# Two attentions on one core: the first use's small tile grows from 32 to 64 bytes, and every tile above it moves by 32

## The chip, the core and the metric

The kernel runs on one core of one Trainium2 chip. The metric is the device time of one execution in microseconds; a figure for a kernel is the median of its runs. Nothing else runs on the core.

## What is computed

Two attention layers with 32 heads of 18 features each, on separate inputs of 2048 rows and 576 features, all in float32. The first (A) is local and dilated: each position looks at 8 positions, 2 apart, behind it. The second (B) is a full softmax attention over all 2048 positions. Each has its own projection to q, k and v and its own output projection, and the two results stand side by side in the output.

```python
def _A_ref(x, wqkv, wo):            # W, dil = 8, 2
    q, k, v = heads(x @ wqkv)
    idx = pos[:, None] - off[None, :]               # off = arange(8) * 2
    logits = einsum("bhsd,bhswd->bhsw", q, k[idx]) * scale   # -1e9 where idx < 0
    return merge(einsum("bhsw,bhswd->bhsd", softmax(logits), v[idx])) @ wo

def _B_ref(x, wqkv, wo):
    q, k, v = heads(x @ wqkv)
    p = softmax(einsum("bhqd,bhkd->bhqk", q, k) * scale)
    return merge(einsum("bhqk,bhkd->bhqd", p, v)) @ wo

return concatenate([A, B], axis=-1)
```

## The kernel before

**Projections.** Operands are split into a high and a low part so that three products in a fast format stand for one in float32. First comes a third of B's q and k columns (L572), then half of B's values (L316), then the rest and all of A's columns in one list of products (L379, inside `stream`). The results go to DRAM and come back in the layout that the next part wants.

**Full attention (B).** It runs in 8 groups of 4 heads; a group has 4 blocks of 512 queries, and a block has 16 steps of 128 keys. A group's q and k lie in a *set*: a tile `qs` and a tile `ks` of 16,384 bytes in each partition. There are three sets, made by `make_set`, and group g uses set g modulo 3. For each pair of queries and keys the scores are made twice:

- L160, in `take`: a product of q and k whose maxima VectorE takes (L168, in `reduce`, out of the PSUM bank into the small tile `mx`). They run about a group ahead; the maxima are transposed, split (`mt`, `mh`) and loaded as two more rows into `qs` (`place`).
- L284, in `score`: the same product with the maximum's rows, now below zero, which ScalarE exponentiates (L292) into a tile `e` of 128 x 512 float32. The keys are the weights, and `qs` is what moves through TensorE.
- L767, in `weigh`: four products of the step's four `e` tiles (moving) with `v` (weights) add up in the bank `po`, one in each quarter of TensorE's columns. A product in plain float32 stands in the trace as two matmuls, so a step shows 8 records.

`finish` divides by the sums; the output projection follows in sums of a few products in between (L1245, L1213, L1177, and at the very end L890).

**Local attention (A)** is done by GpSimd beside B: products of `aq` with windows of `akv` (L988), sums (L992), the exponentials' products with v's windows (L1030) and their sums (L1031 to L1033). Its output projection (L1348) is put between the scores.

**What sets the order.** The instruction order is written by hand: a step's work plus what an agenda (`plan`, `later`) has due in it. Loads and stores are almost all issued from SyncE's queue (L424 and others), some from ScalarE's and GpSimd's. Tiles come from pools; a pool opened with `side="right"` is laid from the high end of a partition's memory, the others one behind another from the low end.

**Where the tiles lie.** From the low end: 8192 bytes that the kernel reserves (L1462), 128 bytes of small constants, `ones` (512 bytes), two tiles `m` of 128 bytes, then set 0 (two tiles of 16,384). That adds up to 41,856, which is 654 times 64. The pool `maxes` begins there, and its first tile is `warm`, of 32 bytes:

```python
    warm = maxes.tile([2, 8], F32, name="warm", bufs=1)     # L397
    nc.scalar.activation(warm, ones[:, :8], AF.Exp)         # L398
```

This instruction is the first use of ScalarE's table of exponentials (the table's load stands in front of it); nothing reads `warm`. Behind it lie `mx`, `v` of even groups, `mt` and `mh`; then, by stages, `first` (the first inputs), the values, sets 1 and 2, half of the `e` tiles (pool `es`), and the pool `work` with the other `e` tiles, `o`, `n`, `y`, `v` of odd groups and all tiles of A. Each takes a multiple of 64 bytes, so that each lies 32 bytes past a multiple of 64. The tiles laid from the high end (inputs `x`, their rows `raw` and `more`, the projections' weights, `ohi`, `olo`) also lie 32 bytes past a multiple of 64, because the high end does.

Of the kernel before, what the change touches and what calls it, by code (L numbers as in the profile page):

```python
# [7 lines left out]
F32 = mybir.dt.float32  # L8
F32R = mybir.dt.float32r
BF16 = mybir.dt.bfloat16  # L10
AF = mybir.ActivationFunctionType
# [50 lines left out]
def two_attentions(ctx: ExitStack, tc, xa, wa, woa, xb, wb, wob, out):  # L62
# [5 lines left out]
    nc = tc.nc  # L68
# [5 lines left out]
    maxes = ctx.enter_context(tc.tile_pool(name="maxes", bufs=1))  # L74
# [24 lines left out]
    ones = const.tile([2, 128], F32, name="ones")  # L99
# [294 lines left out]

    every = slice(0, 512)

    warm = maxes.tile([2, 8], F32, name="warm", bufs=1)  # L397
    nc.scalar.activation(warm, ones[:, :8], AF.Exp)  # L398

    with (tc.tile_pool(name="x", bufs=1, side="right") as xp,  # L400
          tc.tile_pool(name="a0", bufs=1, side="right") as a0):
# [1068 lines left out]
```

## Time and profile before

| | us |
|---|---|
| runs | 1581.26, 1583.42, 1583.88 |
| median | 1583.42 |
| the profiled execution, its own time | 1582.18 |
| its span, from the first to the last instruction | 1579.8 |

The profile is of one execution; its own time is 2.38 us more than its span, and 1.24 us less than the median of the runs. A line of a group of instructions gives the source line, engine, operation, tiles (output <- inputs, without buffer numbers) and shapes, the count, then busy time in us and the mean duration of one in ns, then the engine's idle time in front of them and what ended it. PEld is TensorE's loading of weights, which goes on beside its matmuls. Ends of matmuls are modelled, so that a busy TensorE can hide short waits; the time from one group of steps to the next is the sturdier number.

### The profile page before, as it was taken

How to read it: one execution, taken by the hardware profiler on the slowest of the kernel's cores; microseconds unless marked ns; L12 is line 12 of the kernel's file. 1: busy time of each engine (PE TensorE's matmuls, PEld its weight loads, DVE VectorE, ACT ScalarE, POOL GpSimd, SP SyncE). 2: the span in 40 equal slices, each digit the busy share in tenths (PEclk: the TensorE clock that was granted, in tenths of full speed). 3: DMA queues.
4: the chain of work that ended last, by engine and by line, in shares of the span. 5: the costliest groups of instructions: out<-in, count | busy, mean ns of one | idle time of the engine just before them, and what ended most of it. 6: DMA issues, size and time to landing. Idle time of an engine off the chain costs nothing.

```text
span 1579.8 us, 34955 instructions
## 1 busy us (share of the span) xinstructions
PE 1570.8 (99%) x13272; PEld 940.6 (60%) x13272; DVE 1380.6 (87%) x2333; ACT 1207.4 (76%) x2411; POOL 970.7 (61%) x803
## 2 busy tenths in 40 slices
PE   9999999999999999999999999999999999999998
PEld 7998888999544445445445445444444444545686
DVE  5299999999999999999989999999999999988633
ACT  6424441121699999999999999999999999998654
POOL 2415752210166996996896897797798799682000
PEclk9999999999999999999999999999999999999999
DMA  8948854532312362245326324421721332144311
GB/s 248 241 137 210 270 165 132 145 106 76 66 35 71 71 141 70 73 119 111 74 74 134 90 79 121 118 79 50 152 82 50 91 95 58 50 165 132 140 57 69
DMA packets 188168, 175.65 MB, mean 111 GB/s; under 512 B 119432, under 2 KB 133512, under 8 KB 186272
## 3 DMA queue, kind: packets, MB, share of 16 engines
q1 hardware_dynamic: 182992, 161.73, 36.9%
q0 software_dynamic: 4032, 10.63, 3.2%
q8 instruction: 104, 1.70, 0.5%
q10 hardware_dynamic: 976, 1.07, 0.2%
q14 instruction: 64, 0.52, 0.1%
HBM read 98.77 MB, written 73.47 MB: 109 GB/s over the span
## 4 chain that ended last, share of the span: by engine, by line
PE 97%; DVE 3%; DMA 0%; issue 0%; ACT 0%; SPq 0%; DVEq 0%
PE po L767 30%; PE bank L284 19%; PE bank L160 18%; PE bank L379 17%; PE bank L1348 4%; PE bank L1245 3%; PE bank L572 2%; PE bank L316 2%; DVE mx L168 2%; PE bank L1213 0%; DMA first<-xb 0%; PE bank L1177 0%; PE bank L890 0%; DVE am L1005 0%; DVE o L782 0%
## 5 line engine op out<-in xcount | busy, mean ns | idle before, releaser
L168 DVE TENSOR_REDUCE mx<-bank 128x2 f32<-128x512 f32 x2048 | 1281.8, 684 | 108.4 <-PE bank L160 82.0
L292 ACT ACTIVATE e<-bank 128x512 f32<-128x512 f32 x2048 | 1047.6, 603 | 80.8 <-PE bank L284 78.7
L160 PE MATMUL bank<-ks,qs 54*128 54x512 f32 (+1 forms) x2464 | 787.8, 380 | 2.2 <-DVE mx L168 0.9
L160 PEld LDWEIGHTS bank<-ks,qs 54*128 54x128 f32 x2464 | 402.8, 184 | 392.6 <-DVE mx L168 341.8
L284 PE MATMUL bank<-qs,ks 56*128 56x512 f32 x2048 | 591.3, 425 | 0.6 <-ACT ohi L716 0.6
L767 PE MATMUL po<-e,v 128*19 128x512 f32 x4096 | 531.7, 598 | 0.4
L284 PEld LDWEIGHTS bank<-qs,ks 56*128 56x128 f32 x2048 | 308.7, 184 | 20.8 <-ACT e L292 14.1
L988 POOL TENSOR_TENSOR pr<-aq,akv 128x1024 f32<-128x1024 f32 x72 | 158.5, 2202 | 17.1 <-PE bank L160 14.3
L1030 POOL TENSOR_TENSOR pr<-lg,akv 128x1024 f32<-128x1024 f32 x72 | 158.3, 2199 | 0.6
L767 PEld LDWEIGHTS po<-e,v 128*19 128x19 f32 x4096 | 73.6, 97 | 138.5 <-issue 133.2
L992 POOL TENSOR_TENSOR pr<-pr 128x1024 f32<-128x1024 f32 x64 | 152.7, 2385 | 5.0
L716 ACT ACTIVATE ohi<-bank 128x512 f32<-128x512 f32 (+1 forms) x56 | 30.4, 595 | 151.9 <-issue 126.4
L379 PE MATMUL bank<-xlo,ahi 64*128 64x512 f32 (+1 forms) x448 | 123.5, 387 | 0.0
L379 PE MATMUL bank<-xhi,alo 64*128 64x512 f32 (+1 forms) x448 | 118.7, 387 | 0.0
L379 PE MATMUL bank<-xhi,ahi 64*128 64x512 f32 (+1 forms) x448 | 112.9, 387 | 0.0
L1348 PE MATMUL bank<-wohi,at 64*128 64x288 f32 x480 | 103.3, 304 | 0.0
L1031 POOL TENSOR_TENSOR pr<-pr 128x512 f32<-128x512 f32 x72 | 92.4, 1284 | 5.6
L431 POOL TENSOR_TENSOR alo<-raw,ahi 128x512 fp32r<-128x512 f32 (+1 forms) x14 | 17.6, 1256 | 121.8 <-ACT ahi L430 115.4
L1348 PEld LDWEIGHTS bank<-wohi,at 64*128 64x128 f32 x480 | 74.6, 184 | 27.6 <-ACT e L292 23.8
L526 POOL TENSOR_TENSOR olo<-olo,ohi 128x512 fp32r<-128x512 f32 x36 | 46.2, 1294 | 68.9 <-ACT ohi L525 58.6
L103 POOL CAST mh<-mt 128x32 fp32r<-128x32 f32 x32 | 6.8, 212 | 113.7 <-DVE mt L185 113.7
L379 PEld LDWEIGHTS bank<-xlo,ahi 64*128 64x128 f32 (+1 forms) x448 | 72.0, 182 | 6.0
(210 smaller groups left out, 1866.9 us busy)
## 6 DMA issues: line engine op xcount, KB each, us to landing
do<-n SPq DMA_DIRECT2D x30, 512.0 KB
da<-ohi SPq DMA_DIRECT2D x52, 256.0 KB
akv<-da SPq DMA_DIRECT2D x64, 175.5 KB
out<-y SPq DMA_DIRECT2D x31, 288.0 KB
qs<-dqk SPq DMA_DIRECT2D x30, 288.0 KB
ks<-dqk SPq DMA_DIRECT2D x30, 288.0 KB
at<-dao SPq DMA_DIRECT2D x60, 128.0 KB
rec<-drec SPq DMA_DIRECT2D x29, 256.0 KB
```

The costliest lines, as they stand in the source:

```text
L160: return awaiting(nc.tensor.matmul(ps if part is None else ps[:, 256 * r : 256 * r + 256], qs[at, b, p, 128 * t : 128 * t + 128], ks[at, p ...
L168: nc.vector.tensor_reduce(at, ps.rearrange("q (s n) -> q s n", s=2), axis=AX.X, op=ALU.max)
L284: awaiting(nc.tensor.matmul(ps, ks[at, p, 128 * kt : 128 * kt + 128], qs[at, b, p], start=True, stop=True))
L292: nc.scalar.activation(e, ps, AF.Exp, scale=SCALE)
L379: nc.tensor.matmul(ps, a, b, start=start, stop=stop)
L767: nc.tensor.matmul(po[32 * i : 32 * i + 19], vs[g][:, kt, 19 * i : 19 * i + 19], es[i], start=kt == 0, stop=kt == NT - 1)
L988: nc.gpsimd.tensor_mul(pr, ap(st["q"][:, 2 * c], (SUB, 2), (0, W), (1, SUB)), window(st["k"], c))
L992: nc.gpsimd.tensor_add(st["pr"], st["pr"], pr)
L1030: nc.gpsimd.tensor_mul(at, ap(st["lg"], (0, 2), (SUB, W), (1, SUB)), window(st["v"], c))
L1031: nc.gpsimd.tensor_add(at[:, :, :4], at[:, :, :4], at[:, :, 4:])
L1245: nc.tensor.matmul(sums_[r], *both[r][i], start=i == 0, stop=last)
L1348: return nc.tensor.matmul(ps, a, b, start=r == k == 0, stop=r == 1 and k == len(both[1]) - 1)
```

## The change

`warm` becomes a tile of 16 elements, 64 bytes, and the activation fills all of it:

```diff
-    warm = maxes.tile([2, 8], F32, name="warm", bufs=1)
-    nc.scalar.activation(warm, ones[:, :8], AF.Exp)
+    warm = maxes.tile([2, 16], F32, name="warm", bufs=1)
+    nc.scalar.activation(warm, ones[:, :16], AF.Exp)
```

Every tile behind `warm` from the low end moves up by 32 bytes, onto a multiple of 64: `mx`, `v`, `mt`, `mh`, `first`, the values, sets 1 and 2, all `e` tiles, and all of `work`. What lies in front of it stays, set 0 among them, which already lay on a multiple of 64; what is laid from the high end stays too, 32 bytes past one. The shift is the same for all that move, so distances among them are kept.

On ScalarE, at the very start of the program, the order of instructions reads like this (a minus is the kernel before, a plus the changed one; `first` is the room for the first inputs):

```order
 L1466 UNCONDITIONAL_BRANCH
 L398 ACT_TABLE_LOAD
-L398 ACTIVATE warm<-ones 2x8
+L398 ACTIVATE warm<-ones 2x16
 L424 DMA first<-xb 128x512
 L424 DMA first<-wb 128x2x192
```

No instruction moves: the activation is longer by 8 elements on 2 partitions, and every other row, on every engine, is the same in both, with the same waits.

## The prediction

> **What bounds the kernel now.** I read the page's shares and chain first, to see whose time counts; then the groups; then one stretch for each group of heads, because the kernel before already holds both kinds of tile: set 0 on a multiple of 64 bytes, sets 1 and 2 32 bytes past one. The page:
>
> ```profile
> span 1579.8 us, 34955 instructions
> ...
> PE 1570.8 (99%) x13272; PEld 940.6 (60%) x13272; DVE 1380.6 (87%) x2333; ACT 1207.4 (76%) x2411; POOL 970.7 (61%) x803
> ...
> PE 97%; DVE 3%; DMA 0%; issue 0%; ACT 0%; SPq 0%; DVEq 0%
> PE po L767 30%; PE bank L284 19%; PE bank L160 18%; PE bank L379 17%; PE bank L1348 4%; PE bank L1245 3%; PE bank L572 2%; PE bank L316 2%; DVE mx L168 2%; PE bank L1213 0%; DMA first<-xb 0%; PE bank L1177 0%; PE bank L890 0%; DVE am L1005 0%; DVE o L782 0%
> ```
>
> TensorE is busy for 99% of the span and carries 97% of the chain of waits; transfers, ScalarE and GpSimd carry about nothing. So a tile's place is worth something only if it changes what TensorE takes for a matmul, or makes another engine late enough to stop it. The groups that could:
>
> ```profile
> L168 DVE TENSOR_REDUCE mx<-bank 128x2 f32<-128x512 f32 x2048 | 1281.8, 684 | 108.4 <-PE bank L160 82.0
> L292 ACT ACTIVATE e<-bank 128x512 f32<-128x512 f32 x2048 | 1047.6, 603 | 80.8 <-PE bank L284 78.7
> ...
> L284 PE MATMUL bank<-qs,ks 56*128 56x512 f32 x2048 | 591.3, 425 | 0.6 <-ACT ohi L716 0.6
> L767 PE MATMUL po<-e,v 128*19 128x512 f32 x4096 | 531.7, 598 | 0.4
> ```
>
> Of what moves, TensorE reads sets 1 and 2 (L284, L160), `e` and `v` (L767) and the late tiles of the output projections. Its matmuls on `x` and the weights (L379, L572, L316) read tiles of the high end, which stay.
>
> **The change part by part.**
>
> *The longer activation.* It stands at the very start:
>
> ```profile
> 2.03 0.21 ACT L398 ACTIVATE warm<-ones 2x8 f32<-2x8 f32 x1
> ...
> 4.28 0.52 ACT L430 ACTIVATE whi<-first 128x384 fp32r<-128x384 f32 x1 [2.04 <-DMA first<-wb]
> ```
>
> It takes 0.21 us and ends at 2.24; ScalarE then idles 2.04 us for a transfer. Eight more elements on two partitions cost far less than that: 0. Without the cover it could cost at most what it takes now, 0.2 us.
>
> *Scores and maxima (L284, L160) on sets 1 and 2.* Each block of 16 steps reads rows of 512 elements of `qs`. Groups 3 to 6 have the same work for TensorE (1161 to 1163 matmuls), and use sets 0, 1, 2 and 0 for the scores. These are the stretches of the four groups, each from its first score to the next group's, with every engine's busy time:
>
> ```profile
> core 0: us, PE busy (x) PEld busy (x) DVE busy (x) ACT busy (x) POOL busy (x), PEclk, DMA share, GB/s
> 817.40:958.00 140.60, 140.49 (x1163) 68.50 (x1159) 129.96 (x220) 134.40 (x267) 121.63 (x88) 1.00 0.42 102
> 958.00:1098.30 140.30, 140.21 (x1161) 68.06 (x1157) 129.83 (x221) 133.99 (x266) 115.78 (x83) 1.00 0.35 90
> 1098.30:1239.00 140.70, 140.36 (x1161) 68.14 (x1157) 131.34 (x226) 134.53 (x267) 107.84 (x81) 1.00 0.39 93
> 1239.00:1379.90 140.90, 140.40 (x1161) 67.94 (x1157) 129.55 (x221) 134.10 (x266) 122.96 (x97) 1.00 0.26 73
> ```
>
> And the score matmuls alone (L284) in the same stretches:
>
> ```profile
> 817.40:958.00 140.60, 75.64 (x256) 39.47 (x256) 1.00 0.42 102
> 958.00:1098.30 140.30, 75.48 (x256) 39.29 (x256) 1.00 0.35 90
> 1098.30:1239.00 140.70, 75.44 (x256) 39.34 (x256) 1.00 0.39 93
> 1239.00:1379.90 140.90, 75.34 (x256) 39.30 (x256) 1.00 0.26 73
> ```
>
> The two groups on the aligned set take 140.6 and 140.9 us, the two on shifted sets 140.3 and 140.7. The means differ by 0.25 us, the wrong way for a gain, and less than like groups differ from each other (0.3 and 0.4). Loading `ks` as weights takes 39.3 to 39.5 us in all four. The group on 140.3 is the one in which scores and maxima both mostly read shifted sets, so the maxima hide nothing either. Five groups (1, 2, 4, 5, 7) get an aligned set by the change. The pairs of aligned less shifted go from 140.6 - 140.7 = -0.1 to 140.9 - 140.3 = +0.6 us a group, so the bounds are 5 x -0.1 = -0.5 and 5 x 0.6 = +3.0 us. I take 0, because the scatter among equals covers the difference.
>
> *The products with `e` and `v` (L767).* No `e` lies on a multiple of 64 in this trace. The nearest row is L284, where `qs` also moves through TensorE in rows of 2048 bytes: aligned less shifted goes from 75.34 - 75.48 = -0.14 to 75.64 - 75.44 = +0.20 us on 75.5, that is -0.19% to +0.27%. On 531.7 us that makes -1.0 to +1.4. I take 0, the middle of those rows. `v` is the weights, whose loading lies beside the matmuls.
>
> *What the other engines do with moved tiles.* VectorE's results go 8 bytes at a time to all places of `mx`. GpSimd's windows of `akv` begin, from product to product, 624 bytes on, so that they take four different places within 64 bytes. The rows of these (min/median/max in ns):
>
> ```profile
> L168 DVE TENSOR_REDUCE mx<-bank x2048: 623/682/696, 81.8 to 1491.0; 128x2 f32<-128x512 f32 x187
> ...
> L988 POOL TENSOR_TENSOR pr<-aq,akv x72: 2185/2202/2217, 427.7 to 1329.4; 128x1024 f32<-128x1024 f32 x72
> ...
> L1030 POOL TENSOR_TENSOR pr<-lg,akv x72: 2180/2198/2218, 511.8 to 1404.6; 128x1024 f32<-128x1024 f32 x72
> ```
>
> The 72 products differ by 1.5% from the fastest to the slowest, so the place of an operand is worth no more than that there, and GpSimd is on no chain. VectorE's maxima stand at 682 wherever they go. For both I take 0. ScalarE's writing of `e` has no aligned counterpart; it is a rival below. It is covered as long as ScalarE has time left: in group 3 it is busy 134.4 of 140.6 us, which leaves 6.2 us for 256 activations, 24 ns each.
>
> *Transfers.* The chain holds one, the first inputs into `first`, a tile that moves:
>
> ```profile
> 0.97 3.98 DMA first<-xb
> ```
>
> The loads into `ks` from GpSimd's queue, for set 0 (at 56 us), set 1 (at 159) and set 2 (at 281), land like this:
>
> ```profile
> DMA to landing us min/median/max: 10.5/12.7/14.8
> ...
> DMA to landing us min/median/max: 5.8/6.0/6.8
> ...
> DMA to landing us min/median/max: 4.7/5.9/6.4
> ```
>
> The aligned set is the slowest, because it loads while the other inputs do; sets 1 and 2 lie alike and land alike. A price for the place can't be seen under the load's. The nearest rows for a bound are the medians of sets 1 and 2, which lie alike and differ by 0.1 in 6: on 3.98 us that is 0.07 us either way. I take 0.
>
> On that row the Trainium skill has a rule against this change: "DMA: Bandwidth & Descriptors", section "How a descriptor splits into AXI transactions", says that a descriptor is fetched from the boundary of 256 bytes below its start, and that what lies between costs beats of 32 bytes. By that page a tile that moves up by 32 bytes, and not onto a multiple of 256, costs a beat more for each row: for a row of `y` of 2304 bytes, 72 beats, some 1.4% (an estimate from the page). No run here shows it; by that rule stores get longer that nothing on the chain waits for, and the sum stays the same.
>
> **The sum.** Against the profiled execution's own 1582.18 us (1579.8 of span and 2.38 around it): 0 + 0 + 0 + 0 + 0, so 1582.2. That execution lies 1.2 below the median of the three runs; the middle of all four times (1581.26, 1582.18, 1583.42, 1583.88) is 1582.8, and that is the forecast.
>
> **The rivals.**
>
> *Faster: rows are fetched in pieces of 64 bytes.* A row of 2048 bytes that begins 32 past a multiple touches 33 such pieces, an aligned one 32. If TensorE's reading of `e` were bound by that, L767 would fall by a 33rd: 531.7 / 33 = 16.1 us, and the time would be 1566.7. For it speaks only that no aligned `e` was ever seen. Against it: the same 33rd would be 75.5 / 33 = 2.3 us a group between sets 0 and 1 or 2 in L284, where the rows differ by 0.2 at most, in both directions. 0.11.
>
> *Slower: ScalarE becomes the bound.* If an activation that writes `e` to a multiple of 64 is longer, 24 ns each are hidden, as worked out above (4% of 603); from there on every ns costs 2048 ns. At 30 ns more that is 6 x 2048 = 12.3 us, so 1595. For it: ScalarE is the second busiest engine of these stretches, and this trace shows no wide write of ScalarE at such a place. Against it: no operand on any engine shows a price of place of even 2%. 0.09.
>
> *The change doesn't do what it says:* tiles of the high end remain 32 bytes past a multiple, so that matmuls on `x` keep whatever they pay. They are 21% of the chain (L379, L572 and L316). But those rows hold no sign of a price either, and without one this rival's time is the forecast's, 1582.8. 0.02.
>
> **How the numbers follow.** The forecast, no change beyond scatter, has 0.78. A measurement of this kernel tells about 0.2% (3.2 us) from no change: three runs alone spread over 2.6 us. With the third rival, "within 0.2%" gets 0.80, faster 0.11, slower 0.09. The range takes the bounds: below 1582.8 - 0.5 (scores) - 1.0 (`e`) - 1.5 (from the middle down to the fastest run) = 1579.8; above 1582.8 + 3.0 + 1.4 + 1.1 (up to the slowest run) = 1588.3. I set 1579 to 1588; what is left out are the first two rivals, 0.2 together.
>
> **What would show it.** Right: the four stretches of groups again at 140 to 141 us, L284 again near 75.5 in each, now without a difference of kind; L767 near 531.7 busy; L292 at 603 ns; the chain still 97% TensorE. L767 down to about 516 would prove the first rival; L292 at 627 or more, with ScalarE in the chain, the second. The forecast is wrong if the groups that used set 1 and 2 change and groups 3 and 6 don't, or if all eight change alike: that would be a price of `e`, `v` or `mx` that no row of this trace could show.

## The result, and the profile after

| | before | after |
|---|---|---|
| median of 20 runs, us | 1582.81 | 1585.74 |
| range, us | 1580.93 to 1588.03 | 1584.77 to 1589.31 |
| profiled execution, own time / span | 1582.18 / 1579.8 | 1585.33 / 1583.5 |

The ratio is 1.0019, with a 95% interval of 1.0013 to 1.0026. The change costs 2.9 us. That lies inside the predicted range, but it is more than scatter, and the forecast was none.

The page of the changed kernel, with the rows that answer to those shown of before:

```profile
span 1583.5 us, 34955 instructions
...
PE 1573.9 (99%) x13272; PEld 939.6 (59%) x13272; DVE 1382.0 (87%) x2333; ACT 1207.7 (76%) x2411; POOL 969.8 (61%) x803
...
PE 95%; DVE 3%; DMA 1%; ACT 0%; issue 0%; POOL 0%; SPq 0%; DVEq 0%; POOLq 0%; ACTq 0%
PE po L767 30%; PE bank L284 19%; PE bank L160 18%; PE bank L379 16%; PE bank L1348 4%; PE bank L1245 3%; PE bank L572 2%; PE bank L316 2%; DVE mx L168 2%; DMA raw<-xa 1%; PE bank L1213 0%; ACT e L292 0%; DMA first<-xb 0%; DMA dqk<-olo 0%; PE bank L1177 0%
...
L168 DVE TENSOR_REDUCE mx<-bank 128x2 f32<-128x512 f32 x2048 | 1283.0, 683 | 110.6 <-PE bank L160 83.8
L292 ACT ACTIVATE e<-bank 128x512 f32<-128x512 f32 x2048 | 1047.6, 605 | 80.2 <-PE bank L284 77.8
...
L284 PE MATMUL bank<-qs,ks 56*128 56x512 f32 x2048 | 591.5, 425 | 0.6 <-ACT ohi L716 0.6
L767 PE MATMUL po<-e,v 128*19 128x512 f32 x4096 | 531.8, 598 | 0.4
...
L379 PE MATMUL bank<-xlo,ahi 64*128 64x512 f32 (+1 forms) x448 | 125.7, 392 | 0.0
L379 PE MATMUL bank<-xhi,alo 64*128 64x512 f32 (+1 forms) x448 | 120.6, 391 | 0.0
L379 PE MATMUL bank<-xhi,ahi 64*128 64x512 f32 (+1 forms) x448 | 114.7, 391 | 0.0
```

TensorE's busy time grew by 3.1 us. Of its rows here, those whose durations grew are the last three, the list of products on A's columns, from 387 ns to 391 and 392 (matmuls run side by side there, so that the busy times of such rows overlap and don't add up to the 3.1). Before, the first of them read:

```profile
L379 PE MATMUL bank<-xlo,ahi 64*128 64x512 f32 (+1 forms) x448 | 123.5, 387 | 0.0
```

L767 and L284 stand where they stood (531.7 and 591.3 before). So the operands that moved cost nothing in the attention, and the matmuls that got longer are ones whose operands (`x` and the weights, of the high end) did **not** move. The chain shows one thing more, 1% for a transfer of `xa`'s rows into `raw`.

The four stretches of the prediction, 4.3 us later now (us, then each engine's busy time and its count):

```profile
821.70:962.30 140.60, 140.50 (x1163) 68.52 (x1159) 129.92 (x220) 134.47 (x268) 121.59 (x88) 1.00 0.43 102
962.30:1102.60 140.30, 140.21 (x1161) 68.04 (x1157) 129.75 (x222) 133.94 (x266) 115.69 (x83) 1.00 0.35 90
1102.60:1243.00 140.40, 140.06 (x1161) 68.09 (x1157) 130.95 (x225) 134.21 (x267) 107.53 (x80) 1.00 0.38 92
1243.00:1384.10 141.10, 140.63 (x1165) 67.95 (x1157) 129.74 (x221) 134.25 (x266) 122.95 (x98) 1.00 0.27 74
```

Four groups took 562.5 us before and take 562.4 now. Nothing happens there.

**Where the time came in.** Two groups of L379 in the trace of before, each with its shortest, median and longest duration in ns and its first and last start in us:

```profile
L379 PE MATMUL bank<-xhi,ahi x448: 383/386/434, 200.8 to 410.7; 64*128 64x512 f32 x139, 64*64 64x512 f32 x11
...
L379 PE MATMUL bank<-xhi,whi x192: 386/392/397, 109.3 to 199.6; 64*128 64x512 f32 x192
```

And of after:

```profile
L379 PE MATMUL bank<-xhi,ahi x448: 383/392/443, 201.8 to 415.0; 64*128 64x512 f32 x139, 64*64 64x512 f32 x11
...
L379 PE MATMUL bank<-xhi,whi x192: 386/392/501, 109.2 to 200.7; 64*128 64x512 f32 x192
```

From the first to the last of these products with `ahi` it was 209.9 us, and is 213.2: **3.3 us**, as much as the whole loss. In the part ahead of it, with `whi`, 90.3 became 91.5, which is a wait of its own (below). Windows show how the 3.3 arise, because the count of matmuls in equal windows measures the pace where "busy" can't. Before (the first pair behind the comma is TensorE's busy time and count):

```profile
200.00:240.00 40.00, 40.00 (x349) 33.76 (x348) 39.12 (x64) 14.10 (x26) 18.52 (x17) 1.00 0.51 153
250.00:290.00 40.00, 40.00 (x354) 36.06 (x352) 39.22 (x65) 7.09 (x14) 11.19 (x17) 1.00 0.51 137
290.00:330.00 40.00, 40.00 (x355) 36.05 (x354) 39.03 (x65) 7.93 (x16) 7.05 (x10) 1.00 0.45 128
330.00:370.00 40.00, 40.00 (x354) 36.08 (x352) 39.21 (x65) 9.01 (x18) 4.98 (x7) 1.00 0.33 105
```

After:

```profile
200.00:240.00 40.00, 40.00 (x350) 37.23 (x348) 39.10 (x65) 14.79 (x28) 19.52 (x18) 1.00 0.54 158
250.00:290.00 40.00, 40.00 (x347) 36.57 (x345) 38.81 (x63) 6.96 (x15) 10.45 (x14) 1.00 0.52 135
290.00:330.00 40.00, 40.00 (x346) 34.39 (x344) 38.71 (x63) 8.79 (x18) 7.92 (x12) 1.00 0.48 135
330.00:370.00 40.00, 40.00 (x346) 32.95 (x346) 38.92 (x64) 7.20 (x15) 3.88 (x6) 1.00 0.28 87
```

TensorE is 100% busy at a granted clock of 1.00 in all eight rows. Yet before it did 349 matmuls in 40 us up to 240 us and 354 from 250 on; after, 350 and then 346 or 347. The kernel before had a faster pace in the second part, and the change lost it. In single matmuls the trace turns at 244.0 us: there the maxima (L160), which stand between the L379 products, begin to read set 1 (group 1's block) in place of set 0. In what follows, **part I** is 110 to 244 us (maxima on set 0) and **part II** is 246 to 392 us (maxima on set 1). L379 and L160 use the upper and the lower 64 rows of TensorE in turn, two matmuls side by side (they start some 10 ns apart, and each lasts about 390), so the pace is given as the *pair time*: the time between starts at the two ends of a stretch, divided by half the number of matmuls between. It is worked out from the trace's records of starts, without the wait described below. Before, it was 231.5 ns in part I and 227.8 in part II; after, 231.6 and 232.9. Part II with its two edges has about 667 pairs (152 us at 227.8 ns): 667 x 5.1 ns = 3.4 us.

**Which matmuls slow down.** It isn't the maxima themselves. Between 250 and 400 us, before:

```profile
L160 PE MATMUL bank<-ks,qs 54*128 54x512 f32 x235 | 91.9, 391 | 0.0
...
L379 PE MATMUL bank<-xhi,ahi 64*128 64x512 f32 (+1 forms) x322 | 80.9, 386 | 0.0
```

After:

```profile
L160 PE MATMUL bank<-ks,qs 54*128 54x512 f32 x230 | 89.9, 391 | 0.0
...
L379 PE MATMUL bank<-xhi,ahi 64*128 64x512 f32 x314 | 80.2, 391 | 0.0
```

The maxima, which read the moved set, last 391 ns in both; the products around them, which read nothing that moved, went from 386 to 391. The starts say the same. From a matmul's start to that of the next but one, which uses the same rows, it is 231.7 ns before and 232.2 after for the maxima, and 227.0 and 233.0 for the products (means over part II). Products during which no maximum was in flight are among the slowed ones (226.6 and 233.1), though in most of these the next maximum's weights were being loaded; the 16 in each trace without that either stand at 226.6 and 230.6. So the place of what one matmul in six reads sets the pace of the other five.

**The wait at 189 us.** The chain of after at that place (start, length, what):

```profile
176.05 9.12 DMA raw<-xa
...
185.73 3.83 DMA dqk<-olo
...
189.67 0.60 ACT olo L524
190.27 0.04 issue
190.32 0.51 PE bank L379 x2
```

TensorE waits for `olo`, ScalarE for a store to end, and that for late rows; it costs 1.1 us. The kernel before, run again below, has this wait too, so that nothing ties it to the change.

The bill of the two profiled executions: +1.1 at 189 us, +3.3 in the list of products, -0.65 near 1410 us (before, a wait of L160 for VectorE of 0.6 us stood there), which makes 3.75; the spans differ by 3.7; and what lies around the span is 1.83 us now and was 2.38, so that the own times differ by 3.15.

### The profile page after: what moved, and what is told of

The parts are those of the page before. It is cut to its first block, busy times and chain, and to the rows that moved or that the text cites. A ratio compares the mean times of both kernels' runs of the same rounds, so it can differ in the third digit from the quotient of the medians.

```text
span 1583.5 us, 34955 instructions
## 1 busy us (share of the span) xinstructions
PE 1573.9 (99%) x13272; PEld 939.6 (59%) x13272; DVE 1382.0 (87%) x2333; ACT 1207.7 (76%) x2411; POOL 969.8 (61%) x803
## 4 chain that ended last, share of the span: by engine, by line
PE 95%; DVE 3%; DMA 1%; ACT 0%; issue 0%; POOL 0%; SPq 0%; DVEq 0%; POOLq 0%; ACTq 0%
PE po L767 30%; PE bank L284 19%; PE bank L160 18%; PE bank L379 16%; PE bank L1348 4%; PE bank L1245 3%; PE bank L572 2%; PE bank L316 2%; DVE mx L168 2%; DMA raw<-xa 1%; PE bank L1213 0%; ACT e L292 0%; DMA first<-xb 0%; DMA dqk<-olo 0%; PE bank L1177 0%
## 5 line engine op out<-in xcount | busy, mean ns | idle before, releaser
L160 PE MATMUL bank<-ks,qs 54*128 54x512 f32 (+1 forms) x2464 | 787.9, 380 | 1.5 <-ACT y L1250 0.3
L160 PEld LDWEIGHTS bank<-ks,qs 54*128 54x128 f32 x2464 | 402.6, 184 | 393.0 <-DVE mx L168 341.1
L284 PE MATMUL bank<-qs,ks 56*128 56x512 f32 x2048 | 591.5, 425 | 0.6 <-ACT ohi L716 0.6
L767 PE MATMUL po<-e,v 128*19 128x512 f32 x4096 | 531.8, 598 | 0.4
L284 PEld LDWEIGHTS bank<-qs,ks 56*128 56x128 f32 x2048 | 308.7, 184 | 20.8 <-ACT e L292 14.1
L767 PEld LDWEIGHTS po<-e,v 128*19 128x19 f32 x4096 | 73.6, 97 | 138.5 <-issue 133.2
L379 PE MATMUL bank<-xlo,ahi 64*128 64x512 f32 (+1 forms) x448 | 125.7, 392 | 0.0
L379 PE MATMUL bank<-xhi,alo 64*128 64x512 f32 (+1 forms) x448 | 120.6, 391 | 0.0
L379 PE MATMUL bank<-xhi,ahi 64*128 64x512 f32 (+1 forms) x448 | 114.7, 391 | 0.0
L379 PEld LDWEIGHTS bank<-xlo,ahi 64*128 64x128 f32 (+1 forms) x448 | 72.2, 182 | 6.8
```

The costliest lines, as they stand in the source:

```text
L160: return awaiting(nc.tensor.matmul(ps if part is None else ps[:, 256 * r : 256 * r + 256], qs[at, b, p, 128 * t : 128 * t + 128], ks[at, p ...
L284: awaiting(nc.tensor.matmul(ps, ks[at, p, 128 * kt : 128 * kt + 128], qs[at, b, p], start=True, stop=True))
L379: nc.tensor.matmul(ps, a, b, start=start, stop=stop)
L767: nc.tensor.matmul(po[32 * i : 32 * i + 19], vs[g][:, kt, 19 * i : 19 * i + 19], es[i], start=kt == 0, stop=kt == NT - 1)
```

## The experiments

The theory with which they began: the moved set 1 slows the list of products, by the place of its tiles relative to the tiles that L379 reads at the same time. Rivals: something else that moved (`e`, `v`, `mx`, the transfers); or alignment to 64 bytes as such. Places are given as the distance of a set's tiles from `x`'s tiles, taken modulo 256 bytes: before, 160 for set 0 and 192 for set 1; after, 160 and 224. All edits add pads that nothing reads or writes (a pad of 8 floats is 32 bytes in each partition).

**Set 1 alone.** From the kernel before: set 1 moves by 32 bytes, and what lies behind it by 64, so that it stays 32 past a multiple.

```diff
-                make_set(stack1, 1)
+                stack1.tile([128, 8], F32, name="low_pad"); make_set(stack1, 1); stack1.tile([128, 8], F32, name="high_pad")
```

> The kernel before with set 1 alone moved by 32 bytes, onto a multiple of 64; all else keeps its place within 64 bytes. Theory (phase): in the stretch from 244 to 395 us, where the maxima of L160 read set 1 between the products of L379 on x, a pair of matmuls takes 232.8 ns as in the changed kernel instead of 227.8 as before, since set 1 and x no longer lie alike; 3.3 us more, some 1586.1 us. Rival (another moved tile, or the transfers of the first inputs): nothing changes, 227.8 ns a pair and 1582.8 us.

Measured: 1586.7 us, ratio 1.0025 [1.0014, 1.0036]. Pair times as after: 231.5 and 232.8 ns. Its list of products takes 213.2 us again:

```profile
L379 PE MATMUL bank<-xhi,ahi x448: 383/392/435, 201.4 to 414.6; 64*128 64x512 f32 x139, 64*64 64x512 f32 x11
```

So moving set 1, with what lies behind it, makes the whole loss. That it is set 1 and not what lies behind it, the kernel "set 1 48 / 16" in the table below shows better: there all that lies behind moves by 256 bytes, which changes nothing by itself ("set 1 64 / 0"), and the fast pace is lost as well.

**All but set 1.** The same line put into the changed kernel: set 1 then stands 64 above its place before, 32 past a multiple again; what lies behind it moves by 64 more and stays on multiples, as after.

> The changed kernel with set 1 alone put back to 32 bytes past a multiple of 64. Theory (phase): 227.8 ns a pair from 244 to 395 us, and the time comes back to 1582.8, at most to 1584 if the 1 us that the changed kernel lost at 189 us to a late transfer of raw is due to another moved tile. Rival (another moved tile): 232.8 ns a pair and 1585.7 us.

Measured: 1585.33 us, 1.0017 [1.0008, 1.0026]; pair times 231.5 and 231.4 ns.

```profile
L379 PE MATMUL bank<-xhi,ahi x448: 383/390/430, 204.4 to 416.8; 64*128 64x512 f32 x139, 64*64 64x512 f32 x11
...
PE bank L379 <- ACT olo L524: 2.1, 1, 2.1
```

The first row makes 212.4 us, 2.5 over before. Neither of the two paces that were expected came. A distance of 0 is slow too, but by 3.6 ns a pair and not 5.1. So it isn't that set 1 must not lie on a multiple of 64 bytes: it is 32 past one again, and the fast pace is still gone.

**The high end too.** From the changed kernel, a pad at the high end moves `x`, the weights and the rest there down by 32 bytes: every tile of the kernel then lies on a multiple of 64. Distances: 192 and 0.

```diff
+    ctx.enter_context(tc.tile_pool(name="end", bufs=1, side="right")).tile([128, 8], F32, name="end_pad")
     with (tc.tile_pool(name="x", ...
```

> The changed kernel with the tiles of the high end moved by 32 bytes as well, so that everything lies on multiples of 64. Theory in its relative form (set and x must lie alike): 227.8 ns a pair not only from 244 to 395 us but from 110 to 244 too, where both kernels took 231.5; 134 us less 1.6% is 2.1 us less than before, some 1580.7. Theory in its absolute form (a set at 32 past a multiple is read faster): as the changed kernel, 231.5 and 232.8 ns, 1585.7 us.

Measured: 1582.95 us, 0.9999 [0.999, 1.0007].

```profile
200.00:240.00 40.00, 40.00 (x354) 37.25 (x352) 39.19 (x65) 14.10 (x26) 18.39 (x17) 1.00 0.53 159
250.00:290.00 40.00, 40.00 (x350) 34.96 (x348) 38.95 (x64) 7.10 (x14) 10.22 (x16) 1.00 0.53 137
```

The fast pace has gone over to part I (354 matmuls in 40 us, 228.1 ns), where neither set 0 nor anything in its order changed, only the distance, from 160 to 192. Part II is at 231.4. The gain in part I pays for the loss in part II.

**All 32 past a multiple.** From the kernel before, with set 0 moved by 32 and what lies behind it by 64: set 0 and every tile behind `warm` are then 32 past a multiple of 64, as the high end's are, and the distances are again 192 and 0.

```diff
-    make_set(stack0, 0)
+    stack0.tile([128, 8], F32, name="low_pad"); make_set(stack0, 0); stack0.tile([128, 8], F32, name="high_pad")
```

> The kernel before with set 0 moved by 32 bytes, so that all sets and x lie 32 bytes past a multiple of 64. Theory, in both forms: 227.8 ns a pair from 110 to 244 us instead of 231.5, 2.1 us less than before, some 1580.7. Rival (the place of the set has no part in it): 231.5 ns there, 1582.8 us.

Measured: pair times 227.9 and 231.4 ns, within 0.2 those of the kernel with all on 64. The distance decides them, the alignment doesn't. Its time is 1585.62 us, 1.0015 [1.0005, 1.0024], 2.7 above that kernel's; the profiled execution was its fastest (1582.02) and shows no wait that would tell why. This stays open.

**One tile of the set alone.** `ks` of set 1 moved by 32 with `qs` left (a pad between the two, and one of 24 floats behind them), then `qs` moved by 32, with `ks` 128 above its place (distances 224 and 64).

```diff
+        _ = i == 1 and pool.tile([128, 8], F32, name="mid_pad"); ks = pool.tile(...)   # and high_pad [128, 24]
...
+        _ = i == 1 and pool.tile([128, 24], F32, name="mid_pad"); ks = pool.tile(...)  # and low_pad [128, 8]
```

> The kernel before with the tile ks of set 1 alone moved by 32 bytes; qs of set 1 stays, and all behind it moves by 128. Theory so far: a pair of matmuls between 244 and 395 us takes 227.8, 231.4 or 232.9 ns by the distance, within 128 bytes, of the maxima's operands in set 1 from x (64: 227.8, 96: 232.9, 0: 231.4). If the moving operand of L160 (ks) decides: 232.9 ns, 3.3 us more, 1586.0 us. If its weights (qs) decide: 227.8 ns and 1582.7 us.

> The kernel before with the tile qs of set 1 alone moved by 32 bytes, ks of set 1 and all behind it by 128. If the moving operand decides and only the place within 128 bytes counts: 227.8 ns from 244 to 395 us, 1582.7 us. If the weights decide: 232.9 ns and 1586.0 us. If the place within 256 bytes counts, or a longer period, ks has left it: 231 to 233 ns.

Measured: 1586.0 us, 1.0021 [1.0012, 1.003], part II at 231.6 ns; and 1586.2 us, 1.0026 [1.0016, 1.0036], part II at 232.6 to 232.8 ns. By the pace that is +2.5 and +3.3 us; measured +3.4 and +3.6. Moving `ks`, which moves through TensorE, loses the fast pace by itself. Whether `qs`, the weights, would lose it by itself isn't shown, as the second kernel moved both. But `qs` has a part in the pace: with `ks` at 224, it is 231.6 ns with `qs` at 192 and 232.8 with `qs` at 224 (set 1 alone); with `ks` at 64, it is 232.6 to 232.8 with `qs` at 224 and 231.4 with `qs` at 64 (set 0 8 / 24, in the table below).

**Other distances.** The lines of the first and the fourth experiment with other pads (floats below / behind): set 0 with 8 / 24; set 1 with 24 / 8, 64 / 0 and 48 / 16; set 0 with 8 / 56.

> The kernel before with set 0 moved by 32 bytes and all behind it by 128, so that sets 0 and 1 both lie 64 from x within 128 bytes. Theory (distance within 128): 227.8 ns a pair from 110 to 244 us (before 231.5) and from 244 to 395 us (as before): 2.1 us less than before, 1580.6 us, unless the wait for raw at 189 us, which comes as soon as TensorE runs ahead of that transfer, takes it back: then 1582.7. Rival (period of 256 or more): 231 to 233 ns from 244 to 395 us, some 1583 to 1584 us.

> The kernel before with set 1 moved by 96 bytes and all behind it by 128: the fourth distance, 32 within 128 bytes. Theory: 231.5 ns a pair from 244 to 395 us, as set 0 has it at that distance from 110 to 244 us; 151 us more by 1.6% is 2.4 us, 1585.1 us. If the distance within 64 bytes alone counted, it would be as in the changed kernel, 232.9 ns and 1586.0 us.

> The kernel before with set 1 and all behind it moved by 256 bytes. So far the distance of the maxima's operands from x gave 227.8 ns a pair at 192 within 256 bytes (set 1 of the kernel before, set 0 of the kernels with set 0 moved) and 231.4 at 0 and 64 (set 1 moved by 64 and by 128), so that distances that differ by 64 aren't alike. If the distance within 256 bytes decides: 227.8 ns from 244 to 395 us, as before, 1582.6 us. If the period is longer or the place of the set itself counts: 231.4 ns, 2.4 us more, 1585.0 us.

> The kernel before with set 1 moved by 192 bytes and all behind it by 256: the last distance from x that is a multiple of 64, 128 within 256 bytes. If one distance in four is the fast one: 231.4 ns a pair from 244 to 395 us, 2.4 us more, 1585.0 us. If two are: 227.8 ns and 1582.6 us.

> The kernel before with set 0 moved by 32 bytes and all behind it by 256, so that both sets lie 192 from x within 256 bytes. If the distance within 256 decides: 227.8 ns a pair in both stretches, 110 to 244 and 244 to 395 us. TensorE then runs 1.5 us ahead at 189 us; if the transfer of raw is late there by itself, that gain is lost in its wait and the time is 1582 to 1583; if not, 1580.5 us. If it does not decide: 227.8 and 231.4 ns, some 1585 us as with both sets moved by less.

The pace, and what it makes of the time: 579 pairs in part I (134 us at 231.5 ns) and 667 in part II, times the difference from before's 231.5 and 227.8 (differences of 0.1 are left out as scatter). "Measured" is the median less that of the kernel before, run on the same chip (1582.74, 1582.57 and 1583.02; for the first row 1582.81).

| kernel | distance I, pair ns | distance II, pair ns | by the pace, us | measured, us (median; ratio) |
|---|---|---|---|---|
| after | 160, 231.6 | 224, 232.9 | +3.4 | +2.9 |
| set 1 alone | 160, 231.5 | 224, 232.8 | +3.3 | +4.0 |
| all but set 1 | 160, 231.5 | 0, 231.4 | +2.4 | +2.6 |
| high end too | 192, 228.1 | 0, 231.4 | +0.4 | +0.2 |
| all 32 past | 192, 227.9 | 0, 231.4 | +0.3 | +2.9 |
| set 0 8 / 24 | 192, 227.9 | 64, 231.4 | +0.3 | +2.6 (1585.18; 1.0015 [1.0006, 1.0024]) |
| set 1 24 / 8 | 160, 231.6 | 32, 232.5 | +3.1 | +3.7 (1586.22; 1.0018 [1.0009, 1.0028]) |
| set 1 48 / 16 | 160, 231.6 | 128, 232.6 | +3.2 | +3.1 (1586.1; 1.0018 [1.0009, 1.0028]) |
| set 1 64 / 0 | 160, 231.5 | 192, 227.8 | 0 | -0.1 (1582.94; 0.9995 [0.9986, 1.0005]) |
| set 0 8 / 56 | 192, 227.9 | 192, 227.8 | -2.1 | -1.8 (1581.21; 0.9985 [0.9975, 0.9995]) |

Of the eight distances that are multiples of 32, seven were tried for a whole set (0, 32, 64, 128, 160, 192, 224), and only 192 is fast, in part I as in part II (160 was seen in part I alone, the other slow ones in part II alone). The kernel with set 1 256 higher keeps before's pace in both parts, so a shift by 256 bytes changes nothing:

```profile
200.00:240.00 40.00, 40.00 (x350) 32.60 (x348) 39.11 (x64) 15.22 (x28) 19.79 (x18) 1.00 0.55 161
250.00:290.00 40.00, 40.00 (x354) 33.71 (x352) 39.22 (x65) 7.61 (x16) 10.70 (x15) 1.00 0.53 139
```

And the kernel with both sets at 192 has the fast pace in both:

```profile
200.00:240.00 40.00, 40.00 (x355) 34.88 (x354) 39.21 (x66) 14.73 (x28) 19.42 (x18) 1.00 0.53 159
250.00:290.00 40.00, 40.00 (x354) 34.90 (x352) 39.21 (x66) 7.10 (x14) 11.12 (x17) 1.00 0.52 136
```

It is the one version whose interval lies below the kernel before: 1581.21 us, against 1583.02 for that kernel on the same chip. Its profiled execution (1584.82) was its slowest of ten. The waits of TensorE in it show why that one is long:

```profile
PE bank L160 <- DMA qs<-mt: 1.9, 1, 1.9
...
PE bank L379 <- ACT olo L524: 1.4, 1, 1.4
```

A late transfer into `qs` near 1411 us and the wait at 189 us, both outside the pace.

**The kernel before again**, with no edit, for the scatter of these waits.

> The kernel before, once more, for its profile. If the place of the tiles sets the pace: 231.5 ns a pair from 110 to 244 us and 227.8 from 244 to 395 us again. If the pace is one of two that an execution falls into by chance: 231.4 ns in the second stretch is as likely. If the wait of TensorE for raw at 189 us belongs to the changed kernel: none here; if it comes and goes in any kernel: 0.4 to 2.4 us are possible here too.

Measured: 1582.88 us. Its pair times are 231.6 and 227.8 ns, the same as in its first trace, but now it has the wait at 189 us:

```profile
PE bank L379 <- ACT olo L524: 0.5, 1, 0.5
```

In the fourteen profiled executions the time lost there against the first trace of before runs from 0 to 2.4 us, with no order by what was moved: 1.1 after, 0.7 with set 1 alone, 2.4 with all but set 1, 0.75 in the kernel before again, none in the kernel with 48 / 16. It comes and goes, while the pair times repeat to 0.1 ns or so.

## Why the prediction was wrong

- **What failed** is a step in the part on what bounds the kernel: "Its matmuls on `x` and the weights (L379, L572, L316) read tiles of the high end, which stay", from which their price was left out of the sum. They stay, but the maxima (L160) run among them, on the two halves of TensorE's rows, and read a set that moves. The list got slower as a whole, from 227.8 to 232.9 ns a pair, 3.3 us in all, and the time is lost in the very matmuls that were left out: the products went from 227.0 to 233.0 ns, the maxima only from 231.7 to 232.2.
- The trace of before held the sign. The prediction compared sets in the attention only, where they are indeed equal. In the list of products it didn't compare them: 349 matmuls in 40 us while the maxima read set 0, and 354 while they read set 1. Read so, the two kinds of place differ by 1.4%, in favour of the one that the change takes away.
- **Scores and maxima in the attention**, predicted 0 with bounds of -0.5 and +3.0 us: 0 (562.5 and 562.4 us for the four groups; L284 591.3 and 591.5). That the upper bound equals the loss is chance: it stood for another place.
- **Products with `e` and `v`**, predicted 0: 531.7 and 531.8 us. The rival with rows fetched in pieces of 64 bytes asked for 516, and has fallen.
- **ScalarE's writing of `e`**, predicted no longer than it was: 603 and 605 ns, and 0% in the chain. The rival asked for 627 and more, and has fallen.
- **GpSimd, VectorE, the longer activation**: the maxima's mean is 683 ns, before 684; GpSimd is busy for 969.8 us, before 970.7. Right. For the transfers, set 1 moved alone already makes the loss, and the only transfer that the chain of after adds is late in the kernel before as well. Whether single transfers got longer, as by the rule of the Trainium skill that the prediction cites ("DMA: Bandwidth & Descriptors", section "How a descriptor splits into AXI transactions"), no run here tells apart: packets of 2304 bytes, the size of a row of `y`, have a median of 93 ns in both traces, and a mean of 105.5 before and 107.8 after. But the means spread as far where `y` keeps its place within 256 bytes (106.9 in the kernel before again, 107.8 with "set 1 64 / 0").
- **The third rival**, that the high end's tiles "keep whatever they pay", had the place right, with a chance of 0.02, but not the mechanism: they didn't keep what they paid. Where they are aligned too, the loss is gone (0.9999), yet through another distance of set 0, not through the alignment, as the pair times of the kernel with all tiles 32 past show.

## What stays open

Shown is that the pace of this list hangs on the distance, within 256 bytes, between the set that the maxima read and the high end's tiles that the products read: the fast pace moved with the distance, whichever of the two was moved. Not shown is how: what in TensorE or in the memory meets there, why products slow down that neither read the set nor run beside a maximum, why it is 192 that is fast, and why 0 and 64 cost less than 224, 32 and 128. Near the end of the list, where the weights have 64 columns in place of 128, it goes the other way (some 231 ns a pair before, 228 after). Open too is why the kernels "all 32 past" and "set 0 8 / 24" take 2 to 3 us more than their pace gives. Alignment to 64 bytes alone doesn't explain it: in "set 0 8 / 56" the same tiles are 32 past a multiple, and it takes what its pace gives.

## What to carry to other kernels

When something moves in memory, look at every matmul that runs in the same stretch as one that reads it, not only at those that read it. To find a change of pace on an engine that is 99% busy, count its instructions in equal windows, or take the first and last start of a long list: shares of busy time hide it (100% in all the windows above), and of the modelled durations only the rows of the list show it, by 4 or 5 ns in 387. And when kernels differ by 2 us of 1580, look at a second trace of the same kernel before a wait is put down to the change.

## What was not expected of the hardware

Two streams of 512-column matmuls on TensorE's two row halves, at a clock of 1.00 and with nothing waiting, take 227.8, 231.5 or 232.9 ns a pair, by the distance within 256 bytes between the tiles that one matmul in six reads and the tiles that the others read: 2.2% between the extremes, from 32 bytes. The others slow down, too, and here more than the one in six. Alignment to 64 bytes by itself showed in no engine's durations: pair times agree within 0.2 ns between the kernel with all on 64 and the one with all 32 past, VectorE's maxima take 684 ns before and 683 after, ScalarE's exponentials 603 and 605.
